# Weight loads of the first three experts in halves, and sixteen-byte probability rows loaded later, in an attention and expert-mixture kernel

## The chip, the cores and the metric

One core of one Trainium2 chip. The metric is the time of one execution in microseconds; the profile gives the span of the core's own instructions, which was about 1.7 us shorter than the time for the kernel before.

## The reference

```python
def attn(q, k, v):                      # 8 batches, 8 heads, 576 rows, 64 wide
    k_p, v_p = k, v averaged over groups of 8 rows          # 72 rows each
    return softmax(q @ k_p.T / 8) @ v_p

def moe(x, domain_probs, w1, w2):       # x: 4608 x 512; 4 experts; w1 512x1024, w2 1024x512
    p = domain_probs / (domain_probs.sum(-1, keepdims=True) + 1e-9)
    for e in range(4):
        out += p[:, e:e+1] * (maximum(x @ w1[e], 0) @ w2[e])
```

The output of the first is the input of the second.

## The kernel before

The token rows go through in nine chunks: the first 512 rows of each batch, and a ninth of the 64 rows that remain of each ("the small query rows"). The first chunk begins while weights, keys, values and queries are still being loaded, all through the DMA queue of the POOL engine; they are written as bf16 (the packets of w1's whole rows of 1024 values are of 2048 bytes). The program fixes the order of the instructions on each engine. The parts that the change touches:

```python
def load_w1(e):
    n = 2 if e == 0 else 1                       # only expert 0 in halves
    for i in range(n):
        fs = slice(i * F // n, (i + 1) * F // n)
        for ks in [slice(0, HK), slice(HK, KC)] if n == 2 and i == 0 else [slice(0, KC)]:
            nc.gpsimd.dma_start(out=w1_bf[:, e, ks, fs], in_=moe_w1[e][:, fs]...)

def load_w2(e):
    n = 2 if e in (0, 2) else 1                  # expert 1 whole
    ...
def load_probs():
    # one load for the 8 x 512 rows, two for the small rows, all into p_all
def norm_probs():
    # reduce_sum, add 1e-9, reciprocal, multiply: on all of p_all
```

The order of the loads in POOL's queue, from the start (cut):

```python
load_first(k, ...); load_first(v, ...)           # batch 0, 4 loads each
load_w1(0); load_w1(1); load_probs(); load_w1(2); load_w2(0); load_w1(3)
attention_first()                                # batch 0 on the matmul engine
load_whole(1, k, "kraw"); load_q(1); load_w2(1); load_whole(1, v, "vraw", 2); load_w2(2)
first_chunk()
```

In `attention_first` the pooled values of batch 0 come from matmuls on the loaded rows, in two groups; in `first_chunk` the products of expert 1 follow those of expert 0:

```python
# attention_first
sum_values(0, work); ...; scores_first(0, 1, A2)
sum_values(1, work)                              # needs the last two loads of batch 0's values
turn_half(0, 0, ...); scores_first(1, 1, B2); ...
# first_chunk
scores_of_two(1, 0, 0)
down_plain(0, 1, 0)                              # the first use of w2 of expert 1
```

`down_plain(c, e, r)` is eight matmuls 512 wide, the first four with the first half of the expert's w2, the last four with the second.

The softmax here doesn't subtract the row's maximum and nothing guards it: scores larger than these inputs give would overflow.

## Time and profile before

| | before |
|---|---|
| time, median of 3 | 489.79 us (489.51 to 490.3) |
| span of the profiled run | 488.7 us |
| PE (matmul engine) busy | 480.9 us, 98% |
| DVE (vector) / ACT (scalar) / POOL busy | 78% / 62% / 24% |
| PE's only wait for a changed load | 0.61 us, at 51 us |

A line of the waits reads "engine, tile, line <- who ended the wait: us in total, times, longest". A line of a timeline reads "start, length, engine, line, operation, tiles, count", and in brackets the idle time before it and who ended it. L792 is the matmul of `down_plain`; L314 is that of the sums for batch 0. In the changed kernel these are L796 and L318, because lines were added above them. The lines themselves stand in the prediction.

### The profile page before, as it was taken

How to read it: one execution, taken by the hardware profiler on the slowest of the kernel's cores; microseconds unless marked ns; L12 is line 12 of the kernel's file. 1: busy time of each engine (PE TensorE's matmuls, PEld its weight loads, DVE VectorE, ACT ScalarE, POOL GpSimd, SP SyncE). 2: the span in 40 equal slices, each digit the busy share in tenths (PEclk: the TensorE clock that was granted, in tenths of full speed). 3: DMA queues.
4: the chain of work that ended last, by engine and by line, in shares of the span. 5: the costliest groups of instructions: out<-in, count | busy, mean ns of one | idle time of the engine just before them, and what ended most of it. 6: DMA issues, size and time to landing. Idle time of an engine off the chain costs nothing.

```text
span 488.7 us, 11602 instructions
## 1 busy us (share of the span) xinstructions
PE 480.9 (98%) x4717; PEld 412.2 (84%) x4721; DVE 378.9 (78%) x764; ACT 304.8 (62%) x583; POOL 118.4 (24%) x118
## 2 busy tenths in 40 slices
PE   8999999999999999999999999999999999999996
PEld 4868578898888888888889889888888888888885
DVE  5789899789768976797679866997678766876674
ACT  5787445855676567656765567556755567556650
POOL 8330504242523154016411442111011101110100
PEclk9999999999999999999999999999999999999999
DMA  9999999876966679345945296311112010004003
GB/s 198 209 205 203 201 180 136 99 89 63 113 101 57 88 80 144 34 82 59 160 48 90 27 169 62 68 23 66 34 23 23 23 65 3 12 23 86 1 1 88
DMA packets 101877, 41.98 MB, mean 86 GB/s; under 512 B 73904, under 2 KB 100272, under 8 KB 101824
## 3 DMA queue, kind: packets, MB, share of 16 engines
q0 software_dynamic: 56992, 22.42, 40.4%
q1 hardware_dynamic: 43728, 17.77, 16.7%
q10 hardware_dynamic: 1104, 1.05, 0.6%
q8 instruction: 37, 0.61, 0.5%
q14 instruction: 16, 0.13, 0.1%
HBM read 45.69 MB, written 9.44 MB: 113 GB/s over the span
## 4 chain that ended last, share of the span: by engine, by line
PE 89%; DMA 8%; POOL 2%; issue 0%; DVE 0%; POOLq 0%
PE unit L698 40%; PE o_ps L766 40%; DMA w_bf<-in_moe_w_dram 8%; PE o_ps L792 3%; PE att L463 2%; PE unit L825 1%; POOL wt_bf L144 1%; PE att L388 1%; PE unit L388 1%; POOL w_bf L211 0%; PE att L517 0%; PE att L500 0%; PE unit L481 0%; POOL q_sb L181 0%; PE o_ps L825 0%
## 5 line engine op out<-in xcount | busy, mean ns | idle before, releaser
L842 DVE SCALAR_TENSOR_TENSOR acc<-o_ps,p_all,acc 128x256 f32<-128x256 f32 (+1 forms) x285 | 127.0, 486 | 50.8 <-PE o_ps L766 36.6
L766 PEld LDWEIGHTS <-H 128*128 128x128 bf16 x1320 | 129.1, 98 | 15.0
L698 PEld LDWEIGHTS <-w_bf 128*128 128x128 bf16 x1088 | 105.1, 98 | 13.1 <-DMA w_bf<-in_moe_w_dram 0.4
L678 DVE CUSTOM_DVE_ANT_0 H<-unit,partial 128x512 bf16<-128x512 f32 x128 | 87.3, 685 | 26.4 <-PE unit L698 12.2
L766 PE MATMUL o_ps<-w_bf,H 128*128 128x256 bf16 x792 | 102.6, 273 | 0.0
L698 PE MATMUL unit<-xT,w_bf 128*128 128x256 bf16 x704 | 100.5, 273 | 0.0
L780 POOL TENSOR_TENSOR acc<-acc,addend 128x512 f32<-128x512 f32 x24 | 30.4, 1267 | 255.1 <-ACT addend L778 213.1
L713 ACT COPY partial<-unit 128x512 f32<-128x512 f32 x128 | 72.3, 592 | 30.3 <-PE unit L698 30.2
L698 PEld LDWEIGHTS <-wu_bf 128*128 128x128 bf16 x816 | 77.6, 98 | 11.6 <-issue 2.5
L698 PE MATMUL unit<-xs,wu_bf 128*128 128x256 bf16 x512 | 77.0, 273 | 0.0
L766 PE MATMUL o_ps<-wt_bf,H 128*128 128x256 bf16 x528 | 68.4, 273 | 0.0
L715 ACT ACTIVATE H<-unit 128x512 bf16<-128x512 f32 x66 | 39.8, 605 | 30.9 <-PE unit L698 30.9
L766 PEld LDWEIGHTS <-S 128*128 128x128 bf16 x528 | 51.7, 98 | 6.0
L719 ACT ACTIVATE H<-unit 128x512 bf16<-128x512 f32 x66 | 39.6, 602 | 25.6 <-PE unit L698 25.3
L711 ACT COPY unit<-unit 128x512 f32<-128x512 f32 x68 | 39.4, 582 | 23.6 <-PE unit L698 18.0
L698 PE MATMUL unit<-xs,w_bf 128*128 128x256 bf16 x256 | 38.4, 273 | 0.0
L840 ACT ACTIVATE acc<-o_ps,p_all 128x256 f32<-128x256 f32 x72 | 30.7, 485 | 9.4 <-PE o_ps L766 7.9
L698 PE MATMUL unit<-xT,wu_bf 128*128 128x256 bf16 x240 | 35.7, 272 | 0.0
L154 POOL DMA_DIRECT2D kraw<-in_k_dram x20 | 26.4, 1319 | 36.7 <-DMA kraw<-in_k_dram 36.7
L766 PE MATMUL o_ps<-wt_bf,S 128*128 128x256 bf16 x264 | 34.2, 273 | 0.0
L766 PE MATMUL o_ps<-w_bf,S 128*128 128x256 bf16 x264 | 34.2, 273 | 0.0
L154 POOL DMA_DIRECT2D vraw<-in_v_dram x20 | 29.1, 1454 | 20.4 <-DMA vraw<-in_v_dram 15.2
(157 smaller groups left out, 508.4 us busy)
## 6 DMA issues: line engine op xcount, KB each, us to landing
out_dram<-acc SPq DMA_DIRECT2D x32, 256.0 KB, 4.2
w_bf<-in_moe_w_dram POOLq DMA_DIRECT2D x5, 1024.0 KB, 15.6
q_sb<-in_q_dram POOLq DMA_DIRECT2D x7, 512.0 KB, 9.9
vraw<-in_v_dram POOLq DMA_DIRECT2D x22, 144.0 KB, 6.6
kraw<-in_k_dram POOLq DMA_DIRECT2D x21, 144.0 KB, 5.5
w_bf<-in_moe_w_dram POOLq DMA_DIRECT2D x5, 512.0 KB, 18.2
wt_bf<-in_k_dram POOLq DMA_DIRECT2D x4, 144.0 KB, 5.4
wt_bf<-in_v_dram POOLq DMA_DIRECT2D x4, 144.0 KB, 4.2
```

What stands on the lines that cost most here:

```text
L154: nc.gpsimd.dma_start(out=raw[:], in_=rows_of(src, b, 2 * part, 2 * part + 2), accum_op=ALU.add if part else ALU.bypass)
L678: nc.vector._custom_dve(TENSOR_ADD_SAT, out=dst, in0=ps, in1=part, s0=LARGEST, s1=0.0)
L698: nc.tensor.matmul(ps[:, n * HN:(n + 1) * HN], lhsT=lhs[:, kc, f:f + P], rhs=rhs[:, kc, :], start=(not grows and n == 0 and kc == 0), stop ...
L711: nc.scalar.copy(out=banks[1][:], in_=ps)
L713: nc.scalar.copy(out=part[:, step - 2], in_=ps)
L715: nc.scalar.activation(out=quarter(0, 0), in_=ps, func=ACT.Relu)
L719: nc.scalar.activation(out=quarter(0, 1), in_=ps, func=ACT.Relu)
L766: nc.tensor.matmul(ps[:, j], lhsT=lhs[:, i, j * P:(j + 1) * P], rhs=rhs[:, i, :], start=(not grows and i == 0 and j == 0), stop=(i == HF - 1),
L780: nc.gpsimd.tensor_add(out=dst, in0=dst, in1=addend[:])
L792: nc.tensor.matmul(o_ps, lhsT=lhs, rhs=w2_bf[:, e, fc, :], start=(fc == 0), stop=(fc == FCH - 1), skip_group_check=True,)
L840: nc.scalar.activation(out=dst, in_=o_ps, func=ACT.Copy, scale=prob)
L842: nc.vector.scalar_tensor_tensor(out=dst, in0=o_ps, scalar=prob, in1=dst, op0=ALU.mult, op1=ALU.add,)
```

## The change

The intent: w2 of expert 1 in two loads, so that its product can start with the first half; the same for w1 of experts 1 and 2; and the two small loads of probabilities, 16 bytes per row, out of the early stretch, where the page's DMA row shows 9 (busy 90% or more) in each of the first seven slices of 12.2 us, to a tile of their own that is loaded and normalized in chunk 1 and later, long before the ninth chunk uses it.

```diff
     def load_w1(e):
-        n = 2 if e == 0 else 1
+        n = 2 if e < 3 else 1
...
     def load_w2(e):
-        n = 2 if e in (0, 2) else 1
+        n = 2 if e < 3 else 1
...
+    p_last = const.tile([P, NR, E], F32, name="p_last")
+    def prob_of(c, r, e):
+        return (p_all[:, c * NR + r] if c < B else p_last[:, r])[:, e:e + 1]
     def load_probs():            # the large load alone
...
+    def load_last_probs():       # the two small loads, into p_last
-    def norm_probs():
+    def norm(p, nm):             # as before, on the tile given
...
-        norm_probs()
+        norm(p_all, 0)
...
+            if b == BUSY + 1:
+                put(start + 15, lambda: norm(p_last, 1))
             if b == BUSY:
-                put(start + 5, lambda: load_q_rem(BUSY))
+                put(start + 5, lambda: load_q_rem(BUSY), load_last_probs)
```

More of the change, by code (lines that the diff above doesn't have):

```diff
@@ L205, in load_w1 @@
     def load_w1(e):
-        n = 2 if e == 0 else 1
+        n = 2 if e < 3 else 1
         for i in range(n):
             fs = slice(i * F // n, (i + 1) * F // n)
-            for ks in [slice(0, HK), slice(HK, KC)] if n == 2 and i == 0 else [slice(0, KC)]:
+            for ks in [slice(0, HK), slice(HK, KC)] if e == i == 0 else [slice(0, KC)]:
                 nc.gpsimd.dma_start(
@@ L222, in load_w2 @@
             )
-    NBLK = NCH * NR
+    NBLK = B * NR
     p_all = const.tile([P, NBLK, E], F32, name="p_all")
+    p_last = const.tile([P, NR, E], F32, name="p_last")
+    def prob_of(c, r, e):
+        return (p_all[:, c * NR + r] if c < B else p_last[:, r])[:, e:e + 1]
     def load_probs():
+        nc.gpsimd.dma_start(
+            out=p_all[:].rearrange("p (b r) e -> p b (r e)", r=NR),
+            in_=moe_domain_probs.rearrange("(b s) e -> s b e", s=S)[0:NT].rearrange("(p r) b e -> p b r e", r=NR),
+        )
+    def load_last_probs():
         by_batch = moe_domain_probs.rearrange("(b s) e -> s b e", s=S)
-        nc.gpsimd.dma_start(
-            out=p_all[:, 0:B * NR, :].rearrange("p (b r) e -> p b (r e)", r=NR),
-            in_=by_batch[0:NT].rearrange("(p r) b e -> p b r e", r=NR),
-        )
         for bb in range(2):
-            nc.gpsimd.dma_start(
-                out=p_all[bb * REM:(bb + 1) * REM, B * NR:NBLK, :], in_=by_batch[NT:S, bb::2, :],
-            )
-    def norm_probs():
-        tot = const.tile([P, NBLK], F32, name="tot")
-        nc.vector.reduce_sum(out=tot[:], in_=p_all[:], axis=AX.X)
+            nc.gpsimd.dma_start(out=p_last[bb * REM:(bb + 1) * REM], in_=by_batch[NT:S, bb::2, :])
+    def norm(p, nm):
+        n = p.shape[1]
+        tot = const.tile([P, n], F32, name=f"tot{nm}")
+        nc.vector.reduce_sum(out=tot[:], in_=p[:], axis=AX.X)
         nc.vector.tensor_scalar_add(out=tot[:], in0=tot[:], scalar1=1e-9)
-        inv = const.tile([P, NBLK], F32, name="inv")
+        inv = const.tile([P, n], F32, name=f"inv{nm}")
         nc.vector.reciprocal(out=inv[:], in_=tot[:])
         nc.vector.tensor_tensor(
-            out=p_all[:], in0=p_all[:],
-            in1=inv[:].unsqueeze(2).to_broadcast([P, NBLK, E]), op=ALU.mult,
+            out=p[:], in0=p[:], in1=inv[:].unsqueeze(2).to_broadcast([P, n, E]), op=ALU.mult,
         )
@@ L776, in down @@
             for j in range(BLOCKS):
-                prob = p_all[:, c * NR + row * BLOCKS + j, e:e + 1]
+                prob = prob_of(c, row * BLOCKS + j, e)
                 nc.scalar.activation(out=addend[:, j], in_=ps[:, j], func=ACT.Copy, scale=prob)
@@ L835, in add @@
     def add(o_ps, c, e, r, cols, first):
-        prob = p_all[:, c * NR + r, e:e + 1]
+        prob = prob_of(c, r, e)
         dst = acc[:, r, cols]
```

## The prediction

> **What bounds the kernel now.** I read the page first, then the waits of the matmul engine (PE), then the chain that ended last, then the DMA issues and the timelines of single engines over the first 75 us. From the page, the busy times, the slices and the chain by engine:
>
> ```profile
> span 488.7 us, 11602 instructions
> PE 480.9 (98%) x4717; PEld 412.2 (84%) x4721; DVE 378.9 (78%) x764; ACT 304.8 (62%) x583; POOL 118.4 (24%) x118
> PE   8999999999999999999999999999999999999996
> DMA  9999999876966679345945296311112010004003
> PE 89%; DMA 8%; POOL 2%; issue 0%; DVE 0%; POOLq 0%
> ```
>
> PE is busy 98% of the span, so 488.7 - 480.9 = 7.8 us is all that removing waits can ever give. The DMA row is saturated for the first six slices or so (12.2 us each) and then falls away. The change touches loads only, so the question is where in the first 66 us PE waits for a load. The waits of PE, the whole list over the span:
>
> ```profile
> PE unit L334 <- DVE H L861: 1.3, 1, 1.3
> PE o_ps L792 <- DMA w_bf<-in_moe_w_dram: 0.6, 1, 0.6
> PE att_first L543 <- DVE kpT L306: 0.4, 1, 0.4
> PE att L314 <- DMA wt_bf<-in_k_dram: 0.3, 1, 0.3
> PE o_ps L452 <- DVE x_tok L425: 0.3, 1, 0.3
> PE unit L314 <- DMA wt_bf<-in_v_dram: 0.2, 1, 0.2
> ```
>
> Five of the six fall in the first 15 us, ahead of every load that the change touches (the changed ones land at 20 us and later). The one that remains is 0.6 us, once, for a weight load. The same waits asked from 66 us on gave an empty list: after the first chunk PE never waits for anything the profile names. The timeline shows the place:
>
> ```profile
> 50.35 0.38 PE L388 MATMUL unit<-qT,kpT 64*128 64x256 bf16 x4
> 51.34 1.90 PE L792 MATMUL o_ps<-w_bf,H 128*128 128x512 bf16 x7 [0.61 <-DMA w_bf<-in_moe_w_dram]
> 51.39 0.69 DVE L250 TENSOR_TENSOR wt_bf<-w_bf 128x1024 bf16<-128x1024 bf16 x1 [0.15 <-DMA w_bf<-in_moe_w_dram]
> 53.28 0.75 DVE L842 SCALAR_TENSOR_TENSOR acc<-o_ps,p_all,acc 128x512 f32<-128x512 f32 x1 [0.47 <-PE o_ps L792]
> ```
>
> L792 is the down product of expert 1 in the first chunk; it waits for that expert's w2, loaded whole in one DMA. The vector engine (DVE) waits for the same DMA for 0.15 us and then for PE. The load itself, in the DMA view of the stretch of its issue, and its issue in the timeline of the POOL engine:
>
> ```profile
> 25.44 0.88 POOL L220 DMA_DIRECT2D w_bf<-in_moe_w_dram  x1
> w_bf<-in_moe_w_dram POOLq DMA_DIRECT2D x1, 1024.0 KB, 25.9
> ```
>
> Issued at 25.44, landed 25.9 us later at 51.30 (the landing semaphore in the trace), while PE was ready at 51.34 - 0.61 = 50.73. It was queued 25.9 us but itself moved for only 5.1 us: the load ahead of it in POOL's queue landed at 46.19. So this is a stream that runs in order, and anything removed ahead of it makes it land earlier by that much.
>
> [...]
>
> **The change part by part.**
>
> *1. The two loads of the small rows' probabilities leave the stream.* The trace's landings are: w1 of expert 1 at 23.07, the large probabilities at 23.32, the two small ones at 23.51 and 23.70, then w1 of expert 2 at 28.61. Taking the two away moves everything behind them forward by 23.70 - 23.32 = 0.38 us. On POOL they free 13.00 - 11.75 = 1.25 us of issue early on, worth nothing by itself: the queue is backlogged from there to 66 us. The first normalization then waits for the large load alone: DVE began it at 23.82 and would begin at about 23.4. DVE had no part in a PE wait there.
>
> *2. w1 of experts 1 and 2 in halves.* The rows get half as long (1024-byte instead of 2048-byte packets in bf16), so the cost could rise. Landings: whole loads of 1024 KB took 23.07 - 17.75 = 5.32 us and 28.61 - 23.70 = 4.91 us; the half of expert 0, already split this way, took 17.75 - 15.22 = 2.53 us. Two halves are 5.06 us, against 5.11 as the mean of the two: I take the cost as zero within 0.1 us. What it gains: PE's first use of expert 2's w1 comes at 28.66, the load landed at 28.61 and the matmuls before ended at 28.61; half a load earlier removes 0.05 us. Expert 1's w1 was not waited for, so its split gives nothing.
>
> *3. w2 of expert 1 in halves, the part that matters.* The dry comparison of both programs shows PE's order unchanged, with the first matmul of L792 waiting for the first half and the fifth for the second. The stream's landing of the last byte moves from 51.30 to 51.30 - 0.38 = 50.92, or 50.8 with the 0.1 us of part 2. The first half lands about 2.5 us before, near 48.3. PE arrives at 50.73; its fifth matmul starts 4 x 0.217 = 0.87 us later, at 51.60 (a group of eight 512-wide matmuls starts every 1.73 us in the timeline). Both halves are there in time: the whole 0.61 us goes. With the order alone (no 0.38) the second half would land at 51.30, still 0.3 us before its use, so this step has a double margin.
>
> *4. A further scrap.* The second batch's queries landed at 46.19 and PE used them at 46.24, after matmuls that ended at 46.18; landing 0.4 us earlier removes about 0.06 us.
>
> *5. What the 0.6 us meets afterwards.* DVE finishes its two preceding sums at 51.24, then two weight sums (0.73 us from start to start, 0.69 long) until 52.66. PE's first group would end 0.61 us earlier, at about 52.63, so DVE's accumulation starts 0.6 us earlier too. The next tight place is the values of batch 1, made by DVE at 57.03 for 0.29 us and read by PE's context products that start at 57.18: both shift alike. The attention banks are free (the ACT exponentials end at 52.55, PE would rewrite at 52.80). w2 of expert 2 landed at 55.85 and 58.44 and is used at 59.72. So I keep the gain to the end, because PE runs without a named wait from 66 us.
>
> *6. What is added later.* Two loads of 0.7 us issue each on POOL near 80 us, 1.4 us in all, ahead of the first partial load of the next keys. That chain's last load landed at 103.98 and its reader on DVE starts at 107.43, so 1.4 us fits in 3.4 us. On DVE four more small operations: 4 x 0.2 + 3 x 0.03 = about 0.9 us. The comparison places them just ahead of the sum that started at 148.59; DVE idled 1.42 us right after that sum, so it is back on schedule at the next instruction. Cost on the path: zero.
>
> Sum: 0.61 + 0.05 + 0.06 = 0.72 us at most[...]. I take 0.65 us: 489.79 - 0.65 = 489.14 us, a gain of 0.13%.
>
> **Rivals.** First, the short rows cost more than I think. Packets of 2048 bytes took 177 ns on average between 10 and 66 us, those of 1024 bytes 99 ns, so a byte is 12% dearer by that measure; two experts would take 2 x 5.1 x 0.12 = 1.2 us more, the second half of w2 would land at 52.1 instead of 50.9, the fifth matmul (due 51.6) would wait about 0.5 us, and the time would be 489.6. Against it: the landing of the half that exists already. Second, the semaphore lanes. There are eight for POOL's DMAs, each reused eight loads later, and the issue of a load waits for the one eight before. More loads shift all of these; the second half of w2 of expert 2 now waits for w1 of expert 3 (landed 39.80) instead of 33.67. The queue ahead of it would still hold four loads, enough until about 53 us, so no bubble[...]. Third, the late normalization or the delayed partial loads reach PE: up to 0.9 us back, time about 489.8 to 490. Against it: the idle time named in step 6. Fourth, the gain ends in a DVE wait for values at 57 us; then half is left, 489.5.
>
> **Range and chances.** The best case is 0.72 us, and the runs of the kernel before spread over 0.8 us, so most of my range is noise of a median of a few runs: 488.5 to 489.8. A 2% change would need 9.8 us, more than all of PE's idle time (7.8 us), so faster by over 2% is close to impossible (0.3%); slower needs an ordering accident that no view suggests (0.7%); within 2%: 99%.
>
> **What would show it right or wrong.** Right: the wait of L792 (L796 there) for the weight DMA is gone from PE's list, the two halves land near 48.3 and 50.9, PE's first down product of expert 1 starts near 50.65, the span is 0.6 to 0.7 us shorter, and the idle time after 66 us is the same. Wrong, if the second half lands after 51.6 (rival one), if a load's issue comes so late that the DMA row shows a gap before 66 us (two), if PE gets a wait for DVE near 57 or 150 us, or for keys near 110 us (three, four).

Three things that the text uses can be read in the trace of before. All 34 loads that POOL issued in the first 61 us landed in the order of their issue. Eight semaphores told of those loads in turn, and six issues came 0.28 to 0.29 us after the landing of the load eight before, as at 28.90, 31.42 and 33.96 us after landings at 28.61, 31.13 and 33.67. The reciprocals on 128x4 took 0.18 us and those on 128x8 0.20 us, from which the 0.2 us of step 6 can be estimated.

## The result, and the profile after

Three rounds gave 489.99 us (489.43 to 490.5) against 489.92 us of before in the same rounds, a ratio of 1.0001 with a 95% interval of 0.9988 to 1.0014. A ratio here is the mean time of one kernel's runs over that of the other's of the same rounds, so not quite the ratio of the medians quoted. The prediction was 489.14 us, with a range up to 489.8: wrong.

From the page of the changed kernel:

```profile
span 488.6 us, 11612 instructions
PE 480.8 (98%) x4717; PEld 412.4 (84%) x4721; DVE 379.3 (78%) x768; ACT 304.6 (62%) x583; POOL 120.5 (25%) x121
PE 96%; DMA 1%; POOL 1%; DVE 0%; issue 0%; POOLq 0%
```

The DMA share of the chain that ended last fell from 8% to 1%, as it should if PE no longer waits for the load, yet the span is only 0.1 us shorter. The waits of PE in the changed kernel:

```profile
PE unit L338 <- DVE H L865: 1.3, 1, 1.3
PE unit L318 <- DMA wt_bf<-in_v_dram: 0.9, 1, 0.9
PE att_first L547 <- DVE kpT L310: 0.4, 1, 0.4
PE o_ps L456 <- DVE x_tok L429: 0.3, 1, 0.3
```

The wait for w2 (L792, now L796) is gone. The wait for batch 0's values, 0.2 us before, is 0.9 us. In the timelines of PE, before:

```profile
12.68 0.66 PE L314 MATMUL unit<-wt_bf,S 64*72 64x128 bf16 x17 [0.16 <-DMA wt_bf<-in_v_dram]
```

and in the changed kernel, there and at the down product of expert 1:

```profile
13.37 0.66 PE L318 MATMUL unit<-wt_bf,S 64*72 64x128 bf16 x17 [0.85 <-DMA wt_bf<-in_v_dram]
...
50.91 0.38 PE L392 MATMUL unit<-qT,kpT 64*128 64x256 bf16 x4
51.23 1.90 PE L796 MATMUL o_ps<-w_bf,H 128*128 128x512 bf16 x7
```

PE was 0.69 us later than before at 13 us (13.37 - 12.68) and still 0.50 us later when it came to L796 (51.23 against 51.34 - 0.61 = 50.73). No wait followed there, so it started that product only 0.11 us earlier, at 51.23 instead of 51.34. The last load of batch 0's values had landed at 13.33 instead of 12.64, and it was issued at 7.3 us in both kernels, before the first instruction that the change alters on POOL.

The two halves of w2 in the DMA view of the changed kernel, each in the stretch of its issue (24.96 and 26.48 us):

```profile
w_bf<-in_moe_w_dram POOLq DMA_DIRECT2D x1, 512.0 KB, 23.0
w_bf<-in_moe_w_dram POOLq DMA_DIRECT2D x1, 512.0 KB, 23.8
```

They landed at 47.93 and 50.33 us, both ahead of their use. The late normalization on DVE:

```profile
148.48 0.16 DVE L245 TENSOR_REDUCE tot<-p_last 128x4 f32<-128x16 f32 x1
148.67 0.17 DVE L246 TENSOR_SCALAR tot<-tot 128x4 f32<-128x4 f32 x1
148.88 0.18 DVE L248 RECIPROCAL inv<-tot 128x4 f32<-128x4 f32 x1
149.09 0.18 DVE L249 TENSOR_TENSOR p_last<-p_last,inv 128x16 f32<-128x16 f32 x1
149.18 0.69 DVE L254 TENSOR_TENSOR H<-H 128x1024 bf16<-128x1024 bf16 x1
150.58 0.88 DVE L846 SCALAR_TENSOR_TENSOR acc<-o_ps,p_all,acc 128x256 f32<-128x256 f32 x2 [0.71 <-ACT H L719]
```

It pushed the next sum back by 0.70 us, and the idle time behind that sum shrank from 1.42 to 0.71 us: hidden, as predicted. The list of PE's waits from 66 us on is empty in the changed kernel too.

So the loss is at the start, in a place that the change does not touch. Either the change delays that load by some way not seen, or the load lands early or late by chance and one trace each was too little.

### The profile page after: what moved, and what is told of

It is laid out like the page before. It is cut to its first block, busy times and chain, and to the rows that moved or that the text cites. A ratio compares the mean times of both kernels' runs of the same rounds, so it can differ in the third digit from the quotient of the medians.

```text
span 488.6 us, 11612 instructions
## 1 busy us (share of the span) xinstructions
PE 480.8 (98%) x4717; PEld 412.4 (84%) x4721; DVE 379.3 (78%) x768; ACT 304.6 (62%) x583; POOL 120.5 (25%) x121
## 4 chain that ended last, share of the span: by engine, by line
PE 96%; DMA 1%; POOL 1%; DVE 0%; issue 0%; POOLq 0%
PE unit L702 43%; PE o_ps L770 41%; PE o_ps L796 3%; PE att L467 2%; PE unit L829 1%; DMA wt_bf<-in_v_dram 1%; PE att L392 1%; PE o_ps L621 1%; POOL wt_bf L144 1%; PE unit L621 1%; PE unit L638 1%; PE unit L392 1%; PE o_ps L638 0%; PE att L521 0%; PE att L504 0%
## 5 line engine op out<-in xcount | busy, mean ns | idle before, releaser
L846 DVE SCALAR_TENSOR_TENSOR acc<-o_ps,p_all,acc 128x256 f32<-128x256 f32 (+1 forms) x260 | 115.9, 486 | 43.4 <-PE o_ps L770 32.8
L844 ACT ACTIVATE acc<-o_ps,p_all 128x256 f32<-128x256 f32 x64 | 27.3, 487 | 8.1 <-PE o_ps L770 6.6
```

Of the source, the lines that this page charges most:

```text
L844: nc.scalar.activation(out=dst, in_=o_ps, func=ACT.Copy, scale=prob)
L846: nc.vector.scalar_tensor_tensor(out=dst, in0=o_ps, scalar=prob, in1=dst, op0=ALU.mult, op1=ALU.add,)
```

## The experiments

Eighteen runs of eleven programs were made. Their main reading is one table, put together at the end of this section: when PE came to the down product of expert 1, how long it waited there, and how much time followed.

**again_before**, **again_after**: both kernels unchanged, no edit.

> The kernel before, unchanged: a null run for the noise and a second trace. Theory A (the last load of batch 0's values lands early or late by chance, whatever the kernel, and the changed kernel's profile caught a late one): the landing differs from the 12.64 us of the first trace by some tenths, and PE's wait for it (0.16 us in the first trace) moves with it; the 0.6 us wait for w2 of expert 1 stays. Theory B (the change itself delays that load): it lands within 0.1 us of 12.64 again. Time ratio 1.000 within 0.1%.

> The changed kernel, unchanged, for a second trace and more rounds. Theory A: the landing of batch 0's last values load is drawn anew, PE's wait for it is anywhere from 0 to 0.9 us, and over ten fast runs the mean time is 0.5 to 0.7 us below that of before (ratio 0.9987). Theory B: the load lands at 13.3 us again, PE waits about 0.85 us, ratio 1.000. Theory C (unprofiled runs never had the wait for w2): the trace may differ as in A, the ratio is 1.000.

again_before: 489.89 us, ratio 0.9997 (0.9985 to 1.0009). In its trace PE did not wait for w2 at all:

```profile
50.48 0.38 PE L388 MATMUL unit<-qT,kpT 64*128 64x256 bf16 x4
50.79 1.90 PE L792 MATMUL o_ps<-w_bf,H 128*128 128x512 bf16 x7
```

That is the same program whose first trace shows 0.61 us there. The span was 0.55 us shorter than the first trace's (488.17 against 488.72): the wait, less 0.06 us by which PE came later. again_after: 489.82 us, ratio 0.9996 (0.9983 to 1.0008), the values landed at 12.07 us and PE did not wait for them; it was at L796 at 50.41. So the landing at 13.3 us is not a fixed property of the changed kernel, and the 0.61 us wait is not one of the kernel before. A new theory D: both waits are draws, and the wait for w2 is on average far less than 0.61 us.

**w2_halves**, the part that the prediction counted on, alone, and **w2_whole**, the changed kernel without it:

```diff
 # w2_halves, from the kernel before; w2_whole is the reverse, from the changed kernel
-        n = 2 if e in (0, 2) else 1
+        n = 2 if e < 3 else 1
```

> Before with only w2 of expert 1 in halves; up to 25 us POOL's instructions are those of before. Its halves should land near 48.8 and 51.3, PE has no wait for it, and PE from 52 us on is 0.6 us earlier than in before counted from the end of the start. Theory B: the start is that of before, so the span is 488.1 and the ratio 0.9988. Theory A: the start is drawn anew, the mean ratio is 0.9988 too. Theory C: ratio 1.000.

> The changed kernel with w2 of expert 1 loaded whole again (w1 halves and late probabilities kept). The load should land 0.3 to 0.5 us earlier than in before, against a PE that is there at 50.7 plus what the start lost: wait 0.1 to 0.3 us. Theory B: the start is late as in the changed kernel (load at 13.3 us), ratio 1.0005. Theory A: start drawn anew, ratio 0.9993.

w2_halves: 489.92 us, ratio 0.9998 (0.9986 to 1.0010), no wait for w2, start of the product at 50.41. w2_whole: 490.10 us, ratio 1.0008 (0.9994 to 1.0021); PE came late (50.98) and did not wait for w2, which had landed at 50.38. The intervals are too wide to tell the two apart from before.

**values_first** and **values_first_halves** make the w2 load late on purpose, whole and in halves, to see what halves are worth when they are needed and whether unprofiled runs feel the wait:

```diff
 # both, from the kernel before; the second also has the edit of w2_halves
-        load_w2(1)
         load_whole(1, v, "vraw", 2)
+        load_w2(1)
```

> Before with the two loads of batch 1's values queued ahead of w2 of expert 1, which makes that load about 2.0 us later on purpose [...]. Theory D (w2's landing has almost no wait as a rule: it lands near 50.7, when PE arrives, and the 0.61 us of the first trace was that run's draw): PE waits 1.7 to 2.1 us in the profile and the mean time rises by nearly all of it, 1.7 to 2.0 us, ratio 1.0037. Theory A alone (0.6 us is the standing wait): PE waits about 2.6 us. Theory C (unprofiled runs are far ahead of the load): time rises by less than 1 us though the profile shows the wait.

> The same lateness, but w2 of expert 1 in halves. If halves are worth what the prediction reasoned (the fifth matmul waits, not the first: up to 0.87 us), then PE has no wait before the first matmul, waits 0.9 to 1.2 us before the fifth, and the time is 0.8 to 0.9 us below that of the previous run: ratio to before 1.0020. If halves are worthless, it equals the previous run.

The trace of before shows that the two loads landed at 51.48 and 53.32 us, after w2's 51.30, so the two took 2.02 us.

values_first: 493.29 us, ratio 1.0071 (1.0050 to 1.0091). Timeline of PE:

```profile
53.63 0.56 PE L792 MATMUL o_ps<-w_bf,H 128*128 128x512 bf16 x1 [2.78 <-DMA w_bf<-in_moe_w_dram]
54.41 2.77 PE L792 MATMUL o_ps<-w_bf,H 128*128 128x512 bf16 x6 [0.22 <-issue]
```

The load landed at 53.59, later than I expected. The wait of 2.78 us is far from the 1.7 to 2.1 us of theory D and nearest to theory A's 2.6, so by itself it spoke against D; what speaks for D are the repeated traces. The wait cost more than its length: behind it the matmuls ran at about half rate: from the start of the first to the end of the last recorded one they took 3.55 us, where those of the first trace of before took 1.90. The busy times by stretch, whose columns are stretch, length, busy time (count) of PE, PEld, DVE, ACT and POOL, granted clock, DMA share and GB/s:

```profile
44.00:50.80 6.80, 6.80 (x80) 5.76 (x77) 6.44 (x12) 5.44 (x11) 0.00 (x0) 1.00 1.28 201
53.60:57.00 3.40, 3.15 (x7) 1.00 (x8) 1.39 (x2) 0.00 (x0) 0.00 (x0) 0.52 1.22 195
```

The granted clock was 0.52 for the 3.4 us after the idle time. From the start of the product to the end this kernel took 439.03 us, against 437.37 to 437.40 in the five traces of before: another 1.65 us. Not every run of this kernel lost its clock: three of the six have a mean granted clock of 0.992 to 0.994 and took 493.54 to 495.65 us, the other three 0.998 to 0.999 and 492.23 to 493.05 us.

values_first_halves: 491.49 us, ratio 1.0035 (1.0019 to 1.0051).

```profile
50.73 1.04 PE L792 MATMUL o_ps<-w_bf,H 128*128 128x512 bf16 x3 [0.24 <-DMA w_bf<-in_moe_w_dram]
53.26 1.02 PE L792 MATMUL o_ps<-w_bf,H 128*128 128x512 bf16 x4 [1.49 <-DMA w_bf<-in_moe_w_dram]
```

The wait moved to the fifth matmul, as the mechanism says, and was 1.73 us in all instead of 3.00; the granted clock stayed at 1.00 afterwards, so the gap of 1.49 us did not bring it down. The mean times are 491.76 and 493.57 us: halves save 1.8 us where the load is truly late. About half of that is the clock: the three runs of values_first that kept it average 492.61 us, and against them halves save 0.85 us, close to the 0.87 us between the first matmul and the fifth. (That grouping was made after the runs.) So theory C falls (the timed runs do feel the wait), and the mechanism of the prediction is right. What was wrong is how late the load is as a rule.

**again_before_2**, **again_before_3**, **again_before_4**: three more draws of the kernel before, no edit.

> The kernel before once more, for a third draw of the two waits. Theory D: w2 of expert 1 lands between 50.4 and 51.3, PE's wait for it is 0 to 0.6 us and not 0.6 again, and whatever the span is, the time from PE's thousandth instruction to the end is within 0.05 us of that in the traces so far (387.0 us).

> A fourth draw of the kernel before. Theory D: PE's wait for w2 of expert 1 lies between 0 and 0.6 us (0.61, 0 and 0.19 us so far), and is the smaller, the later the start was. The first reading (a standing wait of 0.6 us): 0.6 us again.

> A fifth draw of the kernel before, with the same expectations as the fourth: a wait for w2 of expert 1 between 0 and 0.6 us by theory D, 0.6 us again by the first reading.

The waits for w2 were 0.19, 0.29 and 0.49 us. From again_before_4:

```profile
51.08 1.25 PE L792 MATMUL o_ps<-w_bf,H 128*128 128x512 bf16 x5 [0.49 <-DMA w_bf<-in_moe_w_dram]
```

With the first two, five draws: 0.61, 0, 0.19, 0.29, 0.49; mean 1.58 / 5 = 0.32 us. That the wait is smaller the later PE comes holds only roughly.

**split_sums**, an attempt at a better kernel: the sums of batch 0's last values in two steps, so that the late load is needed later.

```diff
 # from the changed kernel
-        sum_values(1, work)
+        sum_values_half(0, work[0])
         turn_half(0, 0, chains[1][:])
+        sum_values_half(1, work[1])
         scores_first(1, 1, B2)
```

> The changed kernel, with the last sums of batch 0's values cut in two on PE: those from the load that is early first, then the turn of the first tokens, then those from the last load. If the late landing of that load (12.1 to 13.3 us in six traces) sets the spread of the start, PE's wait for it falls to 0 to 0.6 us instead of 0 to 0.85 us, and the mean time falls by 0.1 to 0.3 us against the changed kernel (ratio to before 0.9994); if cutting the sums costs PE its pairing of two half-height products, it loses 0.3 us instead (1.0006).

490.36 us, ratio 1.0006 (0.9994 to 1.0018): no gain, and nearer the second of the two outcomes, though the interval just reaches the first (0.9994). There was no wait for the values, but 18 products that had run in pairs of half height now came after one another; nine of them took 0.66 us, as all eighteen had before.

**again_after_2** and **w2_halves_2**, repeated on one chip:

> The changed kernel for a third trace and five rounds more on one chip. Theory D: no wait for w2 of expert 1 (halves are immune to the lateness seen so far), the wait for batch 0's last values somewhere in 0 to 0.9 us, ratio between 0.9993 and 1.0000. A standing gain as predicted would give 0.9987.

> Only w2 of expert 1 in halves, again, for five rounds more on the same chip as the run of the changed kernel. Theory D: no wait for that load, ratio as that of the changed kernel (within 0.0008 of it), that is 0.9993 to 1.0000.

490.10 us, ratio 0.9992 (0.9975 to 1.0010), and 490.02 us, ratio 0.9996 (0.9981 to 1.0011). No wait for w2 in either. again_after_2 lost its time at a third place, waiting for w1 of expert 0:

```profile
16.65 0.40 PE L638 MATMUL unit<-xT,w_bf 128*128 128x128 bf16 x4 [0.89 <-DMA w_bf<-in_moe_w_dram]
```

By now kernels with w1 in halves had come to the product at 51.02 us on average (five traces), those with w1 whole at 50.67 (nine). That could be a cost of the change, so it was tried: **w1_whole**, **w1_whole_2** (changed kernel, w1 of experts 1 and 2 whole) and **w1_halves**, **w1_halves_2** (before, with only those halves).

```diff
 # w1_halves, from the kernel before; w1_whole is the reverse, from the changed kernel
-        n = 2 if e == 0 else 1
+        n = 2 if e < 3 else 1
# and, in w1_halves alone, so that only expert 0's first half is cut once more
-            for ks in [slice(0, HK), slice(HK, KC)] if n == 2 and i == 0 else [slice(0, KC)]:
+            for ks in [slice(0, HK), slice(HK, KC)] if e == i == 0 else [slice(0, KC)]:
```

> The changed kernel with w1 of experts 1 and 2 whole again (w2 halves and late probabilities kept). Theory B2 [...]: PE comes to the down product of expert 1 at 50.4 to 50.8 us with no wait there, as in the w2-halves kernel, and the ratio is 0.9993. Theory A2 (chance): arrival anywhere in 50.4 to 51.3.

> Second draw of the kernel with w1 whole: by theory B2 an arrival at 50.4 to 50.8 us again; by theory A2 (chance) anywhere between 50.4 and 51.3 us.

> Before with the w1 halves alone. Theory B2: PE comes late, at 50.9 to 51.3 us, with a wait of 0 to 0.2 us for w2; ratio 1.0005 or above. Theory A2 (chance): arrival anywhere in 50.4 to 51.3 us, with the wait for w2 as in before, ratio 1.0000.

> Second draw of the kernel with only the w1 halves: by theory B2 an arrival at 50.9 to 51.3 us again; by theory A2 (chance) anywhere between 50.4 and 51.3 us.

Theory B2 is that the w1 halves by themselves delay the last load of batch 0's values and w1 of expert 0.

w1_whole: 489.64 us, ratio 0.9994 (0.9981 to 1.0006), arrival at 50.24 and 50.21. w1_halves: 489.97 us, ratio 0.9997 (0.9983 to 1.0011), arrival at 50.20 and 50.50, then a full wait for w2:

```profile
50.86 1.90 PE L792 MATMUL o_ps<-w_bf,H 128*128 128x512 bf16 x7 [0.66 <-DMA w_bf<-in_moe_w_dram]
```

Three of the four arrivals are below 50.4 us, the lowest that had been expected. The w1 halves alone did not make the start late in two traces. What remains is that only kernels with both the w1 halves and the late probabilities had arrivals of 50.98 and later (five of their six traces, the late_after run below corrected by its 0.65 us). The landings show it too: the last load of batch 0's values landed at 12.74 us on average in those six traces and at 12.03 in the fourteen others. I noticed that pattern only afterwards, and no run tests that pair alone. The timed runs don't bear it out: the spans of the changed kernel's 17 runs average 488.0 us, those of w1_whole's five 488.0; less the 437.39 us that follow the start, the 17 runs started the product at 50.6 us on average, and the three traces (50.95) were late ones. So theory B, in the form of a later start on average, is not supported by the times, but no experiment rules it out.

**late_before**, **late_after**: the same added idle work on PE in both kernels (three products, which start 0.216 us apart in the trace of before).

```diff
         up_first(range(4, FCH), second)
+        idle(3, att_first[0][:, 0])
```

> Before with three idle 512-wide products (0.65 us) put into PE's queue near 22 us. If the product of expert 1 starts at the later of PE's arrival and w2's landing (near 51.0 us in before, on average), the wait for w2 is 0 to 0.1 us, PE starts it at 51.2 to 51.5 us, and the time rises by about 0.3 us (ratio 1.0006). If waits simply add, the wait stays near 0.3 us and the time rises by 0.65 us (1.0013).

> The changed kernel with the same 0.65 us of idle products. It has no wait for w2 to take the lateness up, so PE starts the product of expert 1 at 51.0 to 51.9 us without a wait, and the time rises by the full 0.65 us over the changed kernel's 0.9996 of before: ratio about 1.0009, that is equal to the late kernel before or above it.

late_before: 490.19 us, ratio 1.0001 (0.9985 to 1.0018). PE came at 50.94, w2 had landed at 50.97, start at 51.02: the wait was 0.07 us, and the 0.65 us cost 0.06 us in the mean (490.26 against 490.20; 0.26 us if one run of before with 492.35 us at a clock of 0.993 is left out). late_after: 490.38 us, ratio 1.0002 (0.9985 to 1.0019); PE came at 51.85 and started at once. Its mean of 490.46 us is 0.51 us above that of again_after_2 on the same chip. In spans, late_before is 0.1 us above before (488.47 against 488.38 in 43 runs) and late_after 0.6 us above the changed kernel (488.60 against 488.00 in 17). The traces at the product:

```profile
51.02 1.25 PE L793 MATMUL o_ps<-w_bf,H 128*128 128x512 bf16 x5
51.85 1.47 PE L797 MATMUL o_ps<-w_bf,H 128*128 128x512 bf16 x6
```

All this fits the reading that lateness of PE is nearly free in the kernel before and is paid in full in the changed one. It is not shown beyond the noise: the intervals of the ratios overlap, and PE's arrival varies by more than the added 0.65 us from trace to trace, so one trace of each cannot carry it.

The table: PE's arrival at the first matmul of expert 1's down product (its start less the idle time before it), the wait there, the start, and what remained of the span, all in microseconds.

| trace | w2 of expert 1 | arrival | wait | start | rest | span |
|---|---|---|---|---|---|---|
| before | whole | 50.73 | 0.61 | 51.34 | 437.37 | 488.72 |
| again_before | whole | 50.79 | 0 | 50.79 | 437.37 | 488.17 |
| again_before_2 | whole | 50.70 | 0.19 | 50.89 | 437.39 | 488.28 |
| again_before_3 | whole | 50.62 | 0.29 | 50.91 | 437.39 | 488.30 |
| again_before_4 | whole | 50.59 | 0.49 | 51.08 | 437.40 | 488.48 |
| w1_halves | whole | 50.20 | 0.66 | 50.86 | 437.40 | 488.26 |
| w1_halves_2 | whole | 50.50 | 0.60 | 51.09 | 437.38 | 488.48 |
| w2_whole | whole | 50.98 | 0 | 50.98 | 437.39 | 488.37 |
| changed | halves | 51.23 | 0 | 51.23 | 437.39 | 488.61 |
| again_after | halves | 50.41 | 0 | 50.41 | 437.60 | 488.01 |
| again_after_2 | halves | 51.22 | 0 | 51.22 | 437.38 | 488.60 |
| w2_halves | halves | 50.41 | 0 | 50.41 | 437.40 | 487.81 |
| w2_halves_2 | halves | 50.82 | 0 | 50.82 | 437.39 | 488.21 |
| w1_whole | halves | 50.24 | 0 | 50.24 | 437.38 | 487.62 |
| w1_whole_2 | halves | 50.21 | 0 | 50.21 | 437.41 | 487.62 |

What follows the start is the same to 0.04 us in all but one (again_after, 0.2 us more; by the timeline it is lost in two steps of about 0.1 us between 118 and 123 us, each below the 0.15 us from which the profile lists a wait, and its cause was not sought). The start is the later of two things: PE's arrival, drawn between 50.2 and 51.2 us, and, where w2 is whole, its landing, drawn between 50.4 and 51.3. With w2 whole the starts average 50.99 us (eight traces), in halves 50.65 (seven), a gain of 0.34 us; for before and the changed kernel alone they are 51.00 and 50.95.

In the timed runs the changed kernel's three ratios, 1.0001, 0.9996 and 0.9992, average 0.9996, which is 0.2 us. Each interval contains 1, and only the first excludes the predicted 0.9987, barely. All its 17 runs together average 489.91 us; the 46 of before 490.10 (490.05 without the one of 492.35). So a gain of 0.1 to 0.2 us in the time is likely and is not resolved from zero.

The spans say more. The 43 runs of before whose span is on record average 488.38 us (488.32 without the one), the changed kernel's 17 488.00: shorter by 0.3 to 0.4 us, which is what a mean wait of 0.32 us would give. On the two chips that are known to have run both it is 0.20 and 0.39 us (again without the one run). With the spread of the runs, 0.32 us is known to about 0.2 us. Some 0.2 us of it does not reach the time, because the time less the span is 1.73 us for before and 1.91 for the changed kernel. Why is open.

The fastest trace is w1_whole's, and its ratio of 0.9994 is among the lowest, but its interval reaches 1.0006 and one run gave 490.41 us. No version beats both kernels beyond the noise.

## Why the prediction was right or wrong, point by point

- **What bounds the kernel**: right in kind. The only wait that the change can remove is that for w2, and it goes. Wrong in degree: the list of waits of one trace was read as the list of waits of the kernel.
- **Step 1, 0.38 us off the stream**: not separable from the variation between traces. In the changed trace the load after the large probabilities (23.81) landed 2.39 us later, with nothing between; the whole stream was by then 0.4 us later than before (w1 of expert 1 whole at 23.50 instead of 23.07), after the last load of batch 0's values had landed 0.69 us later (13.33 instead of 12.64). In the trace of before the two loads of 4 KB had landed at 23.51 and 23.70, 0.19 us apart.
- **Step 2, w1 halves cost nothing**: right. The two halves of expert 1 took 23.50 - 18.44 = 5.06 us and those of expert 2 28.75 - 23.81 = 4.94 us, and those of w2 of expert 1 50.33 - 45.29 = 5.04 us where the whole had taken 5.11. The first rival, dearer short rows, falls with it. The 0.05 us gain was another draw: that wait was 0, 0.13, 0, 0 and 0.14 us in five traces of before.
- **Step 3, "the whole 0.61 us goes"**: this is the step that failed, by its size. The mechanism held (first half at 47.93, second at 50.33, no wait; values_first_halves shows it at work), but the term is 0.32 us on average over five traces of before, not 0.61, and the spans shrank by 0.3 to 0.4 us. There were two signs. The traced run took 490.43 us, 0.64 above the median of 489.79 from which the prediction subtracted its wait: the sum took a wait seen in a slow run off the time of faster ones. And in the first trace w1 of expert 3 took 39.80 - 33.67 = 6.13 us, where equal loads took 4.9 to 5.3; in the four other traces of before it took 4.93 to 4.99. The stream was about 1 us late in that one run, and some of that was still there when w2 landed.
- **Step 4, 0.06 us**: within the draws, not shown.
- **Step 5, the gain is kept to the end**: right. The rest after the start is constant. But PE's arrival was treated as a fixed 50.73, whereas it varies by 1 us with the landings of batch 0's values and expert 0's w1. In the changed kernel's first trace PE came 0.50 us later, which took back all but 0.11 us of the gain. A second term was missing from the sum: some 0.2 us of the shorter span did not reach the time.
- **Step 6, the later work is free**: right, 0.70 us on DVE where 0.9 was estimated, into idle time. The second, third and fourth rivals did not occur: the issue of the second half of w2 of expert 2 did move from 33.96 to 39.06 us, 0.28 us after w1 of expert 3 had landed at 38.78, as the second said, but the queue had no gap before 66 us that PE waited for, and PE got no wait for DVE or for keys behind 50 us.
- **Range**: it allowed for noise around a sure gain of 0.65 us. The wait's own spread (0 to 0.66) and the arrival's belonged in it. With the mean wait of 0.32 us the centre would have been 489.5 us, but that mean was known only after the repeats. That the first rounds showed no gain at all is partly luck, since over all runs 0.1 to 0.2 us in the time is likely; that the gain falls well short of 0.65 us is not, since the mean wait is half of what was counted on.

Why single landings vary by a microsecond is not settled. The last load of batch 0's values landed between 11.64 and 13.33 us in twenty traces, though it was issued between 7.2 and 7.5 us in all of them. The packet records go with them: in all seven traces where the last load of batch 0's values landed by 11.71 us, no packet of the size of these loads (1152 bytes) took over 0.24 us between 9 and 14 us, but for one of 0.42 us before 9.6; in twelve of the thirteen where it landed at 12.07 us or later, one to five of them took 0.3 to 1.1 us instead of the usual 0.11. That the slow packets are what delayed the load is argued from this and not shown, and why they were slow was not measured.

## What to carry to other kernels

A short wait for a transfer in one trace may be a draw (here 0 to 0.61 us in five traces of one program); before counting on it, profile the same kernel three to five times, compare the traced run's own time with the median (490.43 against 489.79 us here), and look whether equal transfers took equal times in that trace (6.13 us against 4.9 to 5.3). Where a product starts at the later of two arrivals, removing one wait gains the mean excess of one over the other: here the starts were 0.34 us earlier on average, and the mean wait had been 0.32. That lateness of the other, free until then, is then paid fits the spans here (0.65 us of added work made them 0.1 us longer before and 0.6 us after the change), but is not shown beyond the noise. Splitting a load that is consumed in pieces was cheap insurance behind this full queue: two halves took 5.04 us and the whole 5.11, and when the load was really late the split saved 0.85 us against the runs without it that kept their clock, and 1.8 us on average over all.
